# Pooled attention and a squared-ReLU feed-forward: chunk 1's softmax with tokens on partitions, weight splits shared between GpSimd and VectorE, and a unit matrix made by VectorE

## The chip, the core and the metric

The kernel runs on one core of a Trainium2 chip. The time is device microseconds of one execution of the whole program on that core; lower is better. Before the change the runs shown took 985.11, 985.27 and 3297.35 us, median 985.27.

Five engines work in parallel, each through a queue of its own in the order in which the program was written: TensorE (matrix products and transposes, PE in the profile; PEld is its loading of weights), VectorE (DVE), ScalarE (ACT), GpSimd (POOL) and SyncE (SP), which here issues all DMAs.

## What is computed

`B, H, S, D = 8, 8, 576, 64`; the model width is 8 x 64 = 512, there are 4608 tokens and 2048 hidden units. Cut to what matters:

```python
k_p = k.reshape(B, H, S // 8, 8, D).mean(axis=3)          # 72 pooled keys per head
v_p = v.reshape(B, H, S // 8, 8, D).mean(axis=3)
scores = q @ k_p.T / sqrt(D)
scores -= scores.max(axis=-1, keepdims=True)
attn = exp(scores)
attn /= attn.sum(axis=-1, keepdims=True) + 1e-9
x = (attn @ v_p).transpose(0, 2, 1, 3).reshape(4608, 512)
h = maximum(x @ w_in, 0)                                  # w_in 512 x 2048, float64
out = (h * h @ w_out).astype(float32)                     # w_out 2048 x 512, float64
```

q, k and v are float32. The two weight matrices arrive as float64, and are turned into float32 on the chip by bit operations on their 32-bit halves.

## The kernel before, in words

**Chunks, pairs and blocks.** The 4608 tokens go in 12 chunks of 384. A chunk's attention is done for four pairs of heads; pair `p` gives rows `p` of the chunk's `x`, which holds 128 features by 384 tokens for each pair. Then the feed-forward runs in 16 blocks of 128 hidden units, numbered `fc`. `hidden()` (lines 480 to 505) forms the first product of a block into a PSUM tile `h`; ScalarE takes the relu of it, and it is squared. `project()` (517 to 536) forms the second product two blocks later (`LAG = 2`) and adds it into three PSUM tiles `o`, which stay over all 16 blocks.

**Whole and split numbers.** Chunk 0 multiplies whole float32 numbers: four matmuls for a first product (`wf` by `x`, line 487), three for a second. All later chunks multiply split ones: a number is the sum of a high part of type float32r, which ScalarE makes by a copy, and a low part, which VectorE makes by a subtraction (`split`, 111 to 113). Three matmuls, high by high, high by low and low by high, stand for one (489 and 526).

**The way of a weight.** The two matrices lie in 32 keys of 128 x 512 float32: 16 of `w_in`, named `("i", column block, row block)`, and 16 of `w_out`, named `("o", fc)`. For each key the DMA brings the raw words (`land`), ScalarE writes a magnitude (`magnitude`), VectorE makes the float32 value `wf` out of it and the raw words (`to_float32`: two TENSOR_SCALAR and two SCALAR_TENSOR_TENSOR, 147 to 159; two keys that are due in one step are interleaved), and at last `split_weights` makes `wt`, high and low (161 to 163). `need` holds the step of chunk 0 in which a key is wanted, spread to at most `RATE = 2` keys in a step; a key lands `AHEAD` steps ahead of its conversion, and the first `EAGER` land at the start. Line 622 splits key `i` at step `14 + int(0.48 i)`, that is near the end of chunk 0 and in chunk 1.

**Three forms of attention.** Chunk 0 has tokens on partitions (`token_scores`, `token_normalise`, `token_turn`, 403 to 451): scores are 96 tokens by 72 keys, so that maximum and sum run along a partition, on VectorE; then TensorE turns the weights round through PSUM (`pps`), so that keys lie on partitions for the product with V (`weigh_values`). Its exponentials `te` are of scores less their maximum, a subtraction by VectorE. Chunk 1 ("early" in `scores`, 315 to 351) has keys on partitions: GpSimd finds maximum and sum over 72 partitions with PARTITION_ALL_REDUCE (`mx`, `tot`), and the sums make a round through DRAM (`rs`, `rc`, `rr`, `rd`, `rb`) so that VectorE has them on many partitions for the reciprocal. The later chunks do the same, with split K (`kh`, `kl`) and split Q (`st`).

**The order.** Every instruction but those of `make_identity` goes through the helper at line 29, which holds the order of the program; the profile so shows line 29 for nearly all of them, and they are told apart by the names of their tiles. Lines 546 to 609 write chunk 0's attention and the first tasks by hand: loads of K, Q and V of batches 0 and 1, dummy matmuls on `ident` (`keep_busy`), pooling of K by VectorE (`pool_k` for batch 0) and GpSimd (batch 1, `by_halves`), turns of K and Q on TensorE, pooling of V by matmuls with a band matrix `ones` (`pool_v_pair`, six matmuls into `vps`), and the chain from pair to pair. After it comes one loop over all 192 blocks ("steps", 653 to 674). A step issues the first product of its block, then what is due on TensorE, then the second product of two blocks ago, then the other engines' tasks of the step, the weight conversions and splits, and last the relu. What is due when is set by lists: `EARLY` for the attention of chunk 1 and `STEADY` for the later ones (the first step of each pair, and the offsets of its stages), `KV0` and `KV_AT` for loading, pooling and turning the later batches' K and V. A step before -5 counts as -5, and steps -5 to -1 come ahead of chunk 0's first block.

Of the kernel before, what the change touches and what calls it, by code (L numbers as in the profile page):

```python
# [32 lines left out]
def pooled_attn_relu2_ffn(  # L33
# [63 lines left out]
    make_identity(nc, ident)  # L97
# [43 lines left out]
    def magnitude(key):  # L141

        words = raw[key].rearrange("p a (n w) -> p a n w", w=2)
        wf[key] = half_tile("f", "wf_" + "_".join(map(str, key)))
        ACT.activation(wf[key].rearrange("p (a n) -> p a n", a=2), words[..., 1].bitcast(F32), AF.Abs)
# [169 lines left out]
    def scores(c, p):  # L315
# [3 lines left out]
        early = c == 1  # L319
        if early:  # L320

            blocks = st.rearrange("p (i t s) -> p i t s", i=2, s=QT)
            for i in range(2):
                h = 2 * p + i
                for t, (b, _, _) in enumerate(segments(c)):
                    for two in range(2):
                        rows = slice(two * D, (two + 1) * D)
                        PE.matmul(ss[two][:SP_, (i * 2 + t) * QT:(i * 2 + t + 1) * QT], lhsT=kf[b][rows, h // KH, h % KH * SP_:(h % KH + 1) * SP_],
                                  rhs=blocks[rows, i, t, :], start=True, stop=True)
        else:  # L330
            for i in range(2):
                h = 2 * p + i
                for b, o, n in segments(c):
                    kh, kl, _ = kv[b]
                    for j, kk in enumerate((kl, kh)):
                        PE.matmul(ss[i][:SP_, o:o + n], lhsT=kk[:, h * SP_:(h + 1) * SP_], rhs=st[:, i, o:o + n], start=j == 0, stop=j == 1)

        def then():
            if early:
                sc = w_tile(F32, f"sc_{c}_{p}")[:SP_, :, :CH]  # L340
                cols = sc.rearrange("p i (t s two) -> p two i t s", two=2, s=QT)
                for two in range(2):
                    ACT.copy(cols[:, two], ss[two][:SP_, :CH].rearrange("p (i t s) -> p i t s", i=2, s=QT))
            else:
# [360 lines left out]
```

## Time and profile before

| what | value |
|---|---|
| median of the runs shown | 985.27 us |
| the profiled execution | 978.9 us |
| its span, first to last instruction | 977.2 us |
| mean granted clock of TensorE | 0.997 |
| busy: TensorE, its weight loads | 947.3, 785.9 us |
| busy: VectorE, ScalarE, GpSimd | 629.2, 425.8, 401.2 us |
| first matmul of chunk 0's first product | 40.62 us |
| first matmul of chunk 1's first product | 140.10 us |

The profiled execution lies 6.4 us under the median, and its span 1.7 us under its own time. TensorE is busy for 97% of the span, so what another engine does counts only where TensorE waits for it, or where TensorE's own work changes. In the rows of the time line the figures are start, length, engine, instruction, output and inputs; "<-" in brackets names what ended the idle time before an instruction.

### The profile page before, as it was taken

How to read it: one execution, taken by the hardware profiler on the slowest of the kernel's cores; microseconds unless marked ns; L12 is line 12 of the kernel's file. 1: busy time of each engine (PE TensorE's matmuls, PEld its weight loads, DVE VectorE, ACT ScalarE, POOL GpSimd, SP SyncE). 2: the span in 40 equal slices, each digit the busy share in tenths (PEclk: the TensorE clock that was granted, in tenths of full speed). 3: DMA queues.
4: the chain of work that ended last, by engine and by line, in shares of the span. 5: the costliest groups of instructions: out<-in, count | busy, mean ns of one | idle time of the engine just before them, and what ended most of it. 6: DMA issues, size and time to landing. Idle time of an engine off the chain costs nothing.

```text
span 977.2 us, 13363 instructions
## 1 busy us (share of the span) xinstructions
PE 947.3 (97%) x4888; PEld 785.9 (80%) x4888; DVE 629.2 (64%) x1034; ACT 425.8 (44%) x847; POOL 401.2 (41%) x209
## 2 busy tenths in 40 slices
PE   6889989999999999999999999999999999999998
PEld 5544458878888888888888888888888888888997
DVE  5869997886775555776776554777677455453221
ACT  2745457674334344334434434433443434432322
POOL 4398635463444434343435335343534434340000
PEclk9999999999999999999999999999999999999999
DMA  9944203112211002112112001211221100100000
GB/s 244 354 147 163 82 17 98 49 51 82 60 56 49 25 26 74 57 52 87 49 50 74 19 23 60 66 48 36 98 57 43 58 26 17 58 10 9 33 1 32
DMA packets 53361, 64.45 MB, mean 66 GB/s; under 512 B 14936, under 2 KB 34480, under 8 KB 53296
## 3 DMA queue, kind: packets, MB, share of 16 engines
q1 hardware_dynamic: 53296, 63.61, 20.9%
q8 instruction: 38, 0.62, 0.3%
q14 instruction: 27, 0.22, 0.1%
HBM read 53.87 MB, written 9.71 MB: 65 GB/s over the span
## 4 chain that ended last, share of the span: by engine, by line
PE 77%; DVE 13%; issue 5%; ACT 4%; POOL 0%; DMA 0%; POOLq 0%; DVEq 0%; ACTq 0%; SPq 0%
PE o L29 34%; PE h L29 33%; PE sps L29 3%; PE av L29 3%; DVE wf_o L29 3%; DVE wf_i L29 2%; PE qps L29 2%; DVE st L29 2%; DVE r L29 1%; ACT st L29 1%; DVE vp L29 1%; DVE sc L29 1%; ACT gh L29 1%; DVE rb L29 1%; ACT xh L29 1%
## 5 line engine op out<-in xcount | busy, mean ns | idle before, releaser
L29 PE MATMUL h<-xh,w_i 128*128 128x384 f32 x1408 | 389.0, 337 | 0.0
L29 PE MATMUL o<-w_o,gh 128*128 128x512 f32 x1056 | 333.7, 397 | 0.0
L29 POOL PARTITION_ALL_REDUCE tot<-sc x88 | 250.2, 2890 | 192.5 <-issue 179.3
L29 PEld LDWEIGHTS h<-xh,w_i 128*128 128x128 f32 x1408 | 258.7, 188 | 8.4 <-issue 0.5
L29 POOL PARTITION_ALL_REDUCE mx<-sc x88 | 138.2, 1618 | 268.8 <-ACT sc L29 268.8
L29 PE MATMUL h<-xl,w_i 128*128 128x384 f32 x704 | 237.9, 338 | 0.0
L29 PEld LDWEIGHTS o<-w_o,gh 128*128 128x128 f32 x1056 | 193.4, 189 | 32.8 <-issue 1.2
L29 DVE TENSOR_TENSOR gl<-r,gh 128x384 fp32r<-128x384 f32 x176 | 142.6, 810 | 107.8 <-ACT gh L29 107.0
L29 PE MATMUL o<-w_o,gl 128*128 128x512 f32 x528 | 209.0, 396 | 0.0
L29 DVE TENSOR_TENSOR r<-r 128x384 f32<-128x384 f32 x160 | 101.7, 635 | 113.7 <-ACT r L29 113.2
L29 ACT CAST gh<-r 128x384 fp32r<-128x384 f32 x176 | 90.4, 514 | 179.8 <-DVE r L29 179.3
L29 ACT ACTIVATE r<-h 128x384 f32<-128x384 f32 x192 | 94.0, 490 | 106.3 <-PE h L29 105.5
L29 PEld LDWEIGHTS h<-xl,w_i 128*128 128x128 f32 x704 | 132.1, 188 | 8.2 <-issue 0.7
L29 PEld LDWEIGHTS o<-w_o,gl 128*128 128x128 f32 x528 | 99.1, 188 | 22.2
L29 ACT CAST xh<-rb 128x384 fp32r<-128x384 f32 x44 | 22.6, 513 | 136.6 <-DVE rb L29 136.6
L29 DVE TENSOR_TENSOR st<-qps,st 64x384 fp32r<-64x384 f32 x80 | 60.6, 757 | 32.6 <-ACT st L29 32.1
L29 ACT ACTIVATE sc<-sc 72x384 f32<-72x384 f32 x88 | 43.7, 525 | 74.1 <-DVE sc L29 74.1
L29 ACT CAST st<-qps 64x384 fp32r<-64x384 f32 x80 | 59.0, 738 | 0.5
L29 DVE TENSOR_REDUCE vp<-v 72x64 f32<-72x512 f32 x48 | 51.0, 1064 | 0.4
L29 DVE TENSOR_REDUCE kp<-k 96x64 f32<-96x512 f32 x42 | 44.1, 1049 | 3.7 <-DMA k<-in_k_dram 3.7
L29 DVE TENSOR_TENSOR sc<-sc,mx 72x384 f32<-72x384 f32 x88 | 44.5, 545 | 0.0
L29 DVE TENSOR_TENSOR rb<-av,rb 128x384 f32<-128x384 f32 x44 | 24.4, 555 | 30.1 <-PE av L29 29.9
(82 smaller groups left out, 725.9 us busy)
## 6 DMA issues: line engine op xcount, KB each, us to landing
k<-in_k_dram SPq DMA_DIRECT2D x48, 192.0 KB
out_dram<-ob SPq DMA_DIRECT2D x36, 256.0 KB
rb<-rd SPq DMA_DIRECT2D x88, 96.0 KB
raw_i<-in_moe_w_in_dram SPq DMA_DIRECT2D x16, 512.0 KB
raw_o<-in_moe_w_out_dram SPq DMA_DIRECT2D x16, 512.0 KB
v<-in_v_dram SPq DMA_DIRECT2D x48, 144.0 KB
q<-in_q_dram SPq DMA_DIRECT2D x30, 192.0 KB
q<-in_q_dram SPq DMA_DIRECT2D x32, 96.0 KB
```

Source lines behind the costliest of these rows:

```text
L29: return lambda *a, **k: self.tc.keep_in_program_order(f(*a, **k))
```

## The change

It has five parts.

1. VectorE makes `ident`, by a ramp that is doubled five times, a 32 x 32 transpose and four comparisons; before, GpSimd did.
2. In chunk 0, blocks from 6 on (`SPLIT = 6`) form the first product from split weights and a split `x` (`split_x0`, at step 2). Their keys are wanted one step earlier. The second product of chunk 0 stays whole.
3. The split's subtraction goes to GpSimd for those keys whose `need` lies under `HAND` (10 for `w_in`, 8 for `w_out`), 23 of 32, from one step after the conversion on; the others stay on VectorE.
4. Chunk 1 uses the softmax with tokens on partitions, without GpSimd's reductions and the round through DRAM. Its scores and turns take PSUM tiles of the pool `ps_a` (`token_banks`); chunk 0's are `ps_o` and `ps_h` as before. For both chunks ScalarE takes the exponentials straight from PSUM, 72 columns at a time, with minus the scaled maximum as its bias; VectorE's subtraction is gone.
5. Order: K of batch 1 is turned at step 0 and its V pooled at steps 1 to 4, no longer in the part ahead of chunk 0's blocks; V of batch 1 is loaded behind four keys of weights, and the first Q of chunk 1 ahead of them; `EAGER`, `AHEAD`, `EARLY`, `KV0` and `KV_AT` have other values; within a step `weigh_values` comes last of the tasks on TensorE.

```diff
-    make_identity(nc, ident)
+    DVE.memset(ident, 0.0)
+    DVE.memset(ramp[:, 0, :1], 0.0)
+    for n in (1, 2, 4, 8, 16):
+        DVE.tensor_scalar(ramp[:, 0, n:2 * n], ramp[:, 0, :n], float(n), None, op0=ALU.add)
+    DVE.transpose(ramp[:, 1, :], ramp[:, 0, :])
+    for n in range(0, P, 32):
+        rows = slice(n, n + 32)
+        DVE.tensor_scalar(ident[rows, rows], ramp[rows, 0, :], ramp[rows, 1, :1], None, op0=ALU.is_equal)
...
-    FIRST, EAGER, AHEAD = 2, 8, 5
+    FIRST, EAGER, AHEAD = 2, 11, 3
+    SPLIT, HAND = 6, {"i": 10, "o": 8}
-    KV0 = -31
-    EARLY = ((-19, -16, -13, -10), (0, 2, 3, 5, 5, 6, 7, 8))
-    KV_AT = ((0, 1, 2, 3, 4, 5), (2, 3, 4, 5, 6, 7), (5, 8), (6, 7, 8, 9, 10, 11, 12, 13))
+    KV0 = -35
+    EARLY = ((-16, -13, -10, -7), (0, 1, 2, 3, 4))
+    KV_AT = ((0, 1, 4, 5, 8, 9), (2, 3, 6, 7, 10, 11), (7, 12), (12, 13, 16, 17, 20, 21, 24, 25))
...
+    def token_banks(c, p, name, tag):
+        if c:
+            return [ps_a.tile([P, 512], F32, name=f"{name}_{c}_{p}_{j}", tag="a") for j in range(2)]
...
             for i in range(2):
-                DVE.tensor_reduce(m[:, i, 0], views[i], axis=AX.X, op=ALU.max)
+                DVE.tensor_reduce(m[:, 0, i], views[i], axis=AX.X, op=ALU.max)
+                DVE.tensor_scalar(m[:, 1, i], m[:, 0, i], -SCALE, None, op0=ALU.mult)
             for i in range(2):
-                DVE.tensor_tensor(e[i], views[i], m[:, i, 0].unsqueeze(2).to_broadcast([QT, NQ, SP_]), op=ALU.subtract)
-            for i in range(2):
-                ACT.activation(e[i], e[i], AF.Exp, scale=SCALE)
+                for t in range(NQ):
+                    ACT.activation(e[i][:, t], views[i][:, t], AF.Exp, bias=m[:, 1, i, t:t + 1], scale=SCALE)
...
+    def split_x0():
+        xts[0] = [sb.tile([P, NPAIR, CH], F32R, name=f"{x}_0", tag=x, bufs=2) for x in ("xh", "xl")]
+        split(*xts[0], x0[0])
...
-            if c == 0:
-                prods += [(wf[key][:, cols], xts[c][:, cc, :])]
+            if c == 0 and fc < SPLIT:
+                prods += [(wf[key][:, cols], x0[0][:, cc, :])]
...
     for hf in range(2):
-        transpose_k(1, hf)()
+        at(0, transpose_k, 1, hf)
         at(9 + hf, split_k, 1, hf)
+    for p in range(NPAIR):
+        at(1 + p, pool_v_pair, 1, p)
+    at(2, split_x0)
...
-        at(14 + int(i * 0.48), split_weights, key, DVE)
+        if need[key] < HAND[key[0]]:
+            at(max(need[key] + 1, i // 3), split_weights, key, GP)
+        elif key[0] == "i":
+            at(need[key] + 1, split_weights, key, DVE)
+        else:
+            at(max(need[key] + 1, NFC - 1 + late // 2), split_weights, key, DVE)
+            late += 1
```

How the instructions stand in three places, as the compiled programs hold them (helper line 29 before, 28 after). First the start. On GpSimd before, `ident` is made ahead of the band matrix `ones`:

```order
masks.py:197 MEMSET ident 128x128
masks.py:199 ISA
masks.py:199 AFFINE_SELECT ident<-ident 128x128
L29 MEMSET ones 96x432
L29 AFFINE_SELECT ones<-ones 96x432 x2
```

On VectorE after, `ident` stands ahead of the first pooled K tile (`kp`, from the loaded `k`):

```order
L28 MEMSET ident 128x128
L28 MEMSET ramp 128x1
L28 TENSOR_SCALAR ramp<-ramp 128x1
L28 TENSOR_SCALAR ramp<-ramp 128x2
L28 TENSOR_SCALAR ramp<-ramp 128x4
L28 TENSOR_SCALAR ramp<-ramp 128x8
L28 TENSOR_SCALAR ramp<-ramp 128x16
L28 STREAM_TRANSPOSE ramp<-ramp 128x32
L28 TENSOR_SCALAR ident<-ramp 32x32 x4
L28 TENSOR_REDUCE kp_0_162<-k_0_93 96x64
L28 COPY kp_0_162<-kp_0_162 96x64
```

GpSimd's three instructions became twelve of VectorE. Second, TensorE at the end of chunk 0's attention (`av` the product with V, `kps` turned K, `qps` turned Q). Before, K of batch 1 and the first Q of chunk 1 stand ahead of chunk 0's first block, and so do that pair's scores, which follow these rows:

```order
L29 MATMUL vps_3_430<-vv_3_99,ones 72x128 x6
L29 MATMUL av_2_437<-sc_2_420,vp_154 64x384 x2
L29 MATMUL pps_3_0_441<-ident,te_3_382 72x96 x4
L29 MATMUL pps_3_1_442<-ident,te_3_382 72x96 x4
L29 MATMUL av_3_463<-sc_3_451,vp_154 64x384 x2
L29 MATMUL kps_0_468<-ident,kp_0_266 128x96 x3
L29 MATMUL kps_1_473<-ident,kp_3_279 128x96 x3
L29 MATMUL qps_0_484<-ident,q_0_478 128x96 x4
```

After, the first block (`h_0`) follows the last product with V at once:

```order
L28 MATMUL av_2_445<-sc_2_436,vp_169 64x384 x2
L28 MATMUL pps_3_0_449<-ident,te_3_399 72x96 x4
L28 MATMUL pps_3_1_450<-ident,te_3_399 72x96 x4
L28 MATMUL av_3_470<-sc_3_459,vp_169 64x384 x2
L28 MATMUL h_0_497<-x_380,wf_i_0_423 128x384 x4
L28 MATMUL kps_0_506<-ident,kp_0_280 128x96 x3
L28 MATMUL kps_1_510<-ident,kp_3_293 128x96 x3
L28 MATMUL qps_0_514<-ident,q_0_105 128x96 x4
L28 MATMUL h_1_550<-x_380,wf_i_0_423 128x384 x4
L28 MATMUL vps_0_555<-vv_0_110,ones 72x128 x6
```

Turning K and Q moved from ahead of block 0 to behind it, and pooling V of batch 1 (`vps`) to behind block 1. Third, GpSimd during chunk 0's blocks. Before, it has the reductions of chunk 1's softmax behind the pooled K:

```order
L29 TENSOR_TENSOR kp_3_279<-k_4_95 96x64 x2
L29 ISA
L29 ISA mx_0_0_515<-sc_0_512 72x384 x2
L29 ISA tot_0_0_554<-sc_0_512 72x384 x2
L29 ISA mx_1_0_619<-sc_1_616 72x384 x2
L29 ISA tot_1_0_675<-sc_1_616 72x384 x2
L29 ISA mx_2_0_753<-sc_2_750 72x384 x2
L29 ISA tot_2_0_805<-sc_2_750 72x384 x2
```

After, 23 subtractions of the splits stand there, of which these are the last seven, and then the first reduction of chunk 2:

```order
L28 TENSOR_TENSOR w_o_899<-wf_o_782,w_o_899 128x512
L28 TENSOR_TENSOR w_o_968<-wf_o_782,w_o_968 128x512
L28 TENSOR_TENSOR w_i_0_971<-wf_i_0_814,w_i_0_971 128x512
L28 TENSOR_TENSOR w_i_2_1013<-wf_i_0_814,w_i_2_1013 128x512
L28 TENSOR_TENSOR w_o_1016<-wf_o_883,w_o_1016 128x512
L28 TENSOR_TENSOR w_i_0_1072<-wf_i_0_956,w_i_0_1072 128x512
L28 TENSOR_TENSOR w_i_2_1149<-wf_i_0_956,w_i_2_1149 128x512
L28 ISA
L28 ISA mx_0_0_1180<-sc_0_1179 72x384
```

The reductions of chunk 1 are gone from GpSimd, and the splits took their place. On VectorE after, between the sums of chunk 1's pair 2 and the maxima of its pair 3 (`tm_3`, from the scores `sps_3`) stand two interleaved pairs of keys with one subtraction of K's low part (`kl`) between them; the second pair:

```order
L28 TENSOR_TENSOR kl_503<-kf_505,kh_502 128x288
L28 TENSOR_SCALAR wf_i_0_956<-wf_i_0_956 128x512
L28 TENSOR_SCALAR wf_o_996<-wf_o_996 128x512
L28 TENSOR_SCALAR wf_i_0_956<-wf_i_0_956 128x512
L28 TENSOR_SCALAR wf_o_996<-wf_o_996 128x512
L28 SCALAR_TENSOR_TENSOR wf_i_0_956<-raw_i_2_885,wf_i_0_956 128x512
L28 SCALAR_TENSOR_TENSOR wf_o_996<-raw_o_886,wf_o_996 128x512
L28 SCALAR_TENSOR_TENSOR wf_i_0_956<-raw_i_2_885,wf_i_0_956 128x512
L28 SCALAR_TENSOR_TENSOR wf_o_996<-raw_o_886,wf_o_996 128x512
L28 TENSOR_REDUCE tm_3_1115<-sps_3_0_1092 96x4
```

Before, the work between conversions was chunk 1's products and reciprocals; now it is the maxima, sums and normalisation of token softmax.

More of the change, by code (lines that the diff above doesn't have):

```diff
@@ L7 @@
 from concourse import mybir
-from concourse.masks import make_identity
 from concourse._compat import with_exitstack
@@ L555, in pooled_attn_relu2_ffn @@
         load_k(1, i)
-    for p in range(NPAIR):
-        load_v_pair(1, p)
+    load_q(1, 0)
     need = {}
@@ L565, in pooled_attn_relu2_ffn @@
     first_keys = keys[:FIRST]
[L566 removed]
+    for key in keys[:FIRST + 2]:
         land(key)
[L568 removed]
+    for p in range(NPAIR):
+        load_v_pair(1, p)
+    for key in keys[FIRST + 2:EAGER]:
         land(key)
```

115 lines of the change are left out of this document (52 added, 63 removed).

## The prediction

> **What bounds the kernel now.** I read the windows by stage first, then TensorE's waits stage by stage, then the time lines of the first 150 us. Each row of windows gives the stretch, its length, the busy time of the five engines, the granted clock and the DMA.
>
> ```profile
> 0.00:40.60 40.60, 29.48 (x264) 23.68 (x264) 27.56 (x69) 17.59 (x34) 13.17 (x33) 1.00 1.01 289
> 40.60:140.10 99.50, 90.78 (x324) 46.53 (x321) 87.82 (x151) 51.11 (x102) 72.72 (x22) 0.98 0.39 130
> 140.10:215.00 74.90, 73.25 (x366) 60.56 (x365) 62.16 (x98) 51.43 (x101) 37.96 (x15) 1.00 0.20 60
> ```
>
> The kernel has three parts. Until 40.6 us chunk 0's attention runs as a chain through four engines. From 40.6 to 140.1 TensorE does chunk 0's sixteen blocks and is busy 90.8 of 99.5 us, with VectorE at 87.8 just behind it. From 140.1 on TensorE is nearly always busy. The rest is in its waits (the first three rows are of 40 to 150 us, the last of 150 us to the end):
>
> ```profile
> PE h L29 <- ACT r L29: 3.3, 2, 2.1
> PE h L29 <- DVE wf_i L29: 3.0, 5, 0.8
> PE sps L29 <- DVE st L29: 2.3, 1, 2.3
> ...
> PE sps L29 <- DVE st L29: 6.2, 8, 1.7
> ```
>
> So 8.6 us are waited for in chunk 0 and 6.2 in all later chunks. The 2.3 us wait costs more than itself, since the granted clock (column before the last two) then falls to 0.52:
>
> ```profile
> 133.30:135.60 2.30, 0.05 (x1) 0.08 (x2) 1.85 (x3) 2.27 (x5) 0.00 (x0) 1.00 0.10 28
> 135.60:138.00 2.40, 2.40 (x6) 1.58 (x7) 2.30 (x5) 2.34 (x6) 0.56 (x1) 0.52 0.03 7
> 138.00:140.10 2.10, 2.10 (x5) 0.74 (x4) 2.10 (x3) 2.07 (x5) 2.10 (x2) 0.74 0.00 0
> ```
>
> That is 2.40 x 0.48 + 2.10 x 0.26 = 1.7 us lost. Everything the change can win is in the first 140 us and in those 6.2. Nothing in the sixteen-block body of the later chunks is touched but the hours at which K and V are pooled.
>
> **The change, part by part: the start.** The rows are start, length, engine, instruction, and in brackets the idle time before it.
>
> ```profile
> 8.79 1.65 PE L29 MATMUL idle<-ident 128*128 128x128 f32 x6 [8.79 <-POOL ident masks.py:199]
> 10.23 0.69 PE L29 MATMUL kps<-ident,kp 96*128 96x96 f32 x3
> ...
> 6.79 0.19 DVE L29 COPY kp<-kp 96x64 f32<-96x64 f32 x1
> ...
> 36.55 1.57 PE L29 MATMUL av<-sc,vp 72*64 72x384 f32 x4 [0.68 <-ACT sc L29]
> 38.05 0.71 PE L29 MATMUL kps<-ident,kp 96*128 96x96 f32 x6
> ...
> 40.62 2.85 PE L29 MATMUL h<-x,wf_i 128*128 128x384 f32 x8
> ```
>
> TensorE waits for GpSimd's ident until 8.79 and turns K at 10.23, though the third pooled tile was ready at 6.98. VectorE is idle until 3.47 us, when its first K lands; twelve tiny instructions fit there, so making ident costs nothing. If K landed at once they would cost some 2 us. The gain is at most 10.23 - 6.98 = 3.2 us. Then the chain from pair to pair rules: exponentials now read PSUM in eight pieces (slower for ScalarE), but VectorE's subtraction is gone; I let these cancel. The new banks rule adds a wait: a pair's scores go into banks that ScalarE's exponentials of an earlier pair still read, with that pair's transposes queued behind on TensorE. I take 0.5 us off for it: the last values end at 38.1 - 2.7 = 35.4 (bounds 34.9 and 38.1). Pooling V of batch 1, now behind the start, lay in gaps of this chain; taking it out gains nothing there. In SP's queue V of batch 1 moves behind four weight loads and chunk 1's first Q ahead of them; it is now wanted some 25 us later, so I price this at nothing. Without that slack it would be the wait for one such load.
>
> **TensorE's work in chunk 0.** Starts of neighbouring groups give what each takes:
>
> ```profile
> 22.53 1.53 PE L29 MATMUL vps<-vv,ones 96*72 96x128 f32 x12
> 23.89 0.82 PE L29 MATMUL pps<-ident,te 96*72 96x96 f32 x8
> 24.65 1.22 PE L29 MATMUL sps<-kf,st 64*96 64x72 f32 x16
> ...
> 93.79 1.45 PE L29 MATMUL h<-x,wf_o 128*128 128x384 f32 x4
> ...
> 96.37 2.74 PE L29 MATMUL o<-wf_i,r 128*128 128x512 f32 x6
> 98.94 1.45 PE L29 MATMUL h<-x,wf_o 128*128 128x384 f32 x4
> ...
> 160.38 0.33 PE L29 MATMUL h<-xh,w_i 128*128 128x384 f32 x1
> ...
> 162.48 0.62 PE L29 MATMUL o<-w_o,gh 128*128 128x512 f32 x2
> ```
>
> A first product takes 96.37 - 93.79 = 2.58 us with whole weights and 162.48 - 160.38 = 2.10 with split ones, three matmuls for each old one; a second product takes 98.94 - 96.37 = 2.57. Ten blocks change: -4.8. Four V poolings come in from the start, 4 x 1.36 = +5.4. Four pairs of token turns are new, 4 x 0.76 = +3.0. Turning K and Q and the first scores of chunk 1 move behind block 0, 40.62 - 38.05 = +2.6. TensorE thus has 6.2 us more here. Its old work is 90.8 - 1.7 = 89.1. Without any wait chunk 1 would begin at 35.4 + 89.1 + 6.2 = 130.7 in place of 140.1. The waits decide what is left of those 9.4 us.
>
> **VectorE and GpSimd.** The first four rows are one run of VectorE and the pause after it; the next two what GpSimd and SP's queue did meanwhile. Then GpSimd's additions by shape (busy, mean ns), a 96x8 instruction of VectorE beside such additions and the same alone, and the weight conversions of the stage.
>
> ```profile
> 46.56 1.41 DVE L29 TENSOR_SCALAR wf_i<-wf_i 128x512 f32<-128x512 f32 x4
> 50.31 1.41 DVE L29 TENSOR_SCALAR wf_o<-wf_o 128x512 f32<-128x512 f32 x4
> 57.20 0.67 DVE L29 SCALAR_TENSOR_TENSOR wf_i<-raw_o,wf_i 128x512 uint32<-128x512 uint32 x1
> 65.49 0.17 DVE L29 TENSOR_SCALAR rr<-rc 96x8 f32<-96x8 f32 x1 [7.61 <-DMA rc<-rs]
> ...
> 46.81 15.95 POOL L29 PARTITION_ALL_REDUCE tot<-sc  x2 [1.67 <-ACT sc L29]
> ...
> 60.29 2.74 SPq L29 DMA_DIRECT2D rs<-tot  x2
> ...
> L29 POOL TENSOR_TENSOR k<-k 96x256 f32<-96x256 f32 x6 | 4.3, 720 | 5.8 <-DMA k<-in_k_dram 5.8
> L29 POOL TENSOR_TENSOR k<-k 96x128 f32<-96x128 f32 x6 | 2.8, 469 | 0.5
> ...
> 26.17 0.46 DVE L29 TENSOR_SCALAR tm<-tm 96x8 f32<-96x8 f32 x1
> ...
> 30.53 0.17 DVE L29 TENSOR_SCALAR tm<-tm 96x8 f32<-96x8 f32 x1
> ...
> L29 DVE TENSOR_SCALAR wf_o<-wf_o 128x512 f32<-128x512 f32 x15 | 8.7, 612 | 2.6 <-ACT wf_o L29 2.4
> L29 DVE TENSOR_SCALAR wf_i<-wf_i 128x512 f32<-128x512 f32 x14 | 8.7, 652 | 0.0
> L29 DVE TENSOR_SCALAR wf_i<-wf_i 128x512 uint32<-128x512 uint32 x14 | 8.3, 627 | 0.1
> L29 DVE TENSOR_SCALAR wf_o<-wf_o 128x512 uint32<-128x512 uint32 x15 | 7.9, 562 | 0.0
> ```
>
> Two keys take VectorE 50.31 - 46.56 = 3.75 us undisturbed, 0.35 of it per TENSOR_SCALAR. Over the stage 58 of these took 33.6 us, 13 more than 58 x 0.35: they were held up by GpSimd. The reverse is stronger. GpSimd's sum that was issued at 46.81 sent its result only at 60.29, 2.4 us after VectorE's run ended at 57.9; the run itself kept its pace. [...]
>
> Of GpSimd's new work, 23 splits of 128x512, no row stands here. From 0.720 and 0.469 the step is 0.25 per 128 columns, so 1.22 us each, 28 in all (estimate). [...] VectorE gives up 23 splits, but only three of the 32 stood in this stage before, all at its end; so this relieves the next stage and not this one. Token softmax costs it about as much as the old subtractions and products, since the reciprocal's round trip (7.61 us idle at 65.49, and 2.1 us of TensorE's wait) goes. New are x's low half over 1536 columns (four times a 384-column subtraction, about 2) and four V copies (1). VectorE so needs about 88 + 3 = 91 us, less some 6 for keys that are due after the last gating one, plus some 5 of waits for ScalarE; it starts at about 36.5, is done with block 14's weights at about 126.5, and TensorE has some 10 us left from there (two blocks of 2.10, two second products, a pair's scores): 136.5. ScalarE gets 25 casts forward from the next stage and holds chunk 1's exponentials, ordered ahead of the relu of a block: a late maximum on VectorE keeps a PSUM bank from being freed. I add 1. Chunk 1 begins at 137.5, that is 130.7 + 6.8 us of waits: 2.6 earlier.
>
> [...]
>
> **After 140 us.** 21 splits leave VectorE's next stage and K and V are pooled over twice as many blocks, both of which thin what stands ahead of st on VectorE. Of the 6.2 us of waits I take 3 as gone (bounds -6 and +4, since new hours can meet GpSimd's reductions).
>
> **The sum.** -2.6 - 3 = -5.6 us: span 971.6, profiled execution 973.3. The profiled execution before took 978.9 with a span of 977.2; the median of the runs shown is 985.27, 6.4 us above. I carry the difference over: 985.27 - 5.6 = 979.7, or 980.
>
> **Rivals.** (1) Forecast, waits of 4 to 11 us in chunk 0: 975 to 984, chance 0.48. (2) The splits cost VectorE nearly nothing, since its pauses for ScalarE and TensorE take them: waits of 1 to 3 us, chunk 1 at 132 to 134, and 4 us later on: 985.3 - 7.5 - 4 = 974, 968 at best; for it, GpSimd loses its 72.7 us of reductions in this stage; against it, VectorE's load; 0.24. (3) Slower: GpSimd is locked out, as at 46.81. [...] Blocks 8, 10 and the turns then wait 3 to 6 us each, with clock losses of 1.7 behind the longest: 14 to 21 us of waits. It is slower from 9.4 + 3 = 12.4 us on, 987 to 994; 0.18. (4) The new hours of K and V collide and cost 0.5 us in each of ten chunks: 988; 0.05. (5) It doesn't do what it says at the start, because Q and not ident holds the first transposes: 983; 0.05.
>
> About 2% (20 us) is what a measurement of this kernel tells from no change. Faster than that needs the whole 9.4, all 6.2 and 4 more: 0.03. Slower needs case 3 at its worst beside case 4: 0.03. Within 2%: 0.94. The range leaves out some 0.08 at each side, the best end of case 2 and the worst of case 3: 969 to 993.
>
> **What would show it.** Right: the first K transposes near 7 us, chunk 0's first product near 35, chunk 1's between 134 and 142, VectorE's conversions with single lengths over 1 us beside a split. Wrong: first products that wait for GpSimd's w_i by more than 4 us together (case 3), or splits of 1.2 us with no VectorE row stretched (case 2); a start later than 38 us; more than 6.2 us of waits after 150 us.

## The result: 1.4% slower

The changed kernel took 998.74 us in the median (998.34 to 1000.13) beside 985.19 us of the kernel before: a ratio of 1.0142, interval 1.0122 to 1.0162. Measured a second time it was 997.67 beside 984.57 us, 1.0141 [1.0099, 1.0184]. The prediction was 980 us with a range of 969 to 993: the sign was wrong, and the time lies outside the range.

I cut both traces at two marks: the first matmul of chunk 0's first product, and the first second product of chunk 1 ("the mark" from here on). In each row stand the stretch, its length, the busy time of TensorE, its weight loads, VectorE, ScalarE and GpSimd, and then the granted clock and the DMA. The windows of the changed kernel:

```profile
0.00:46.85 46.85, 37.29 (x190) 27.16 (x191) 27.97 (x76) 18.98 (x52) 12.70 (x31) 0.74 0.99 283
46.85:181.73 134.88, 116.84 (x524) 75.59 (x523) 107.84 (x195) 78.17 (x169) 63.42 (x31) 0.91 0.27 88
181.73:998.40 816.67, 812.90 (x4250) 714.16 (x4248) 488.33 (x773) 341.19 (x676) 300.02 (x153) 1.00 0.15 47
```

The same of the kernel before:

```profile
0.00:40.62 40.62, 29.50 (x264) 23.68 (x264) 27.58 (x69) 17.61 (x34) 13.17 (x33) 1.00 1.00 289
40.62:153.17 112.55, 103.83 (x379) 55.64 (x377) 97.50 (x168) 58.04 (x116) 78.70 (x24) 0.98 0.37 125
153.17:977.20 824.03, 813.99 (x4251) 706.58 (x4249) 504.08 (x799) 350.15 (x698) 309.35 (x152) 1.00 0.15 47
```

The start lost 6.2 us, chunk 0 lost 22.3, and all behind the mark gained 7.4: together 21.2 in one look at each. (A look is one execution.) That is more than the 13.6 us between the medians, since the look at the kernel before lies 6.3 us under its median and the one at the changed kernel 1.4 above. Two looks at the changed kernel gave spans of 998.4 and 995.9, and 134.88 and 132.22 us for chunk 0, so less than 3 us of a single look is not read; where the clock at the start comes out otherwise, it can be more (chunk 0's first product came at 40.62 us in one look at the kernel before and at 46.25 in another with an edit that does not touch the start). Chunk 1's first product, forecast at 137.5 us, came at 168.69.

Of the 22.3 us of chunk 0, 13.0 are TensorE being busy longer and 9.3 TensorE waiting longer (18.0 against 8.7). The granted clock of 0.74 and 0.91 says at once that the busy time is not all new work. Weighted with the granted clock in slices of 0.1 us, the busy time is 106.5 us of full speed against 102.1: 4.4 us are work and 8.6 are clock. TensorE's waits from 40 to 165 us in the changed kernel (total, times, longest):

```profile
PE pps L28 <- DVE te L28: 9.8, 4, 4.5
PE av L28 <- ACT te L28: 5.3, 1, 5.3
PE h L28 <- ACT r L28: 3.0, 3, 1.2
PE av L28 <- ACT sc L28: 1.3, 2, 1.0
```

The waits are in chunk 1's softmax: its turns (`pps`) wait for VectorE's normalisation, and one product with V (`av`) for ScalarE's exponentials. Behind the mark TensorE waits for nothing at all; the kernel before waited 6.2 us there.

### The profile page after: what moved, and what is told of

It is laid out like the page before. It is cut to its first block, busy times and chain, and to the rows that moved or that the text cites. A ratio compares the mean times of both kernels' runs of the same rounds, so it can differ in the third digit from the quotient of the medians.

```text
span 998.4 us, 13540 instructions
## 1 busy us (share of the span) xinstructions
PE 967.0 (97%) x4960; PEld 816.9 (82%) x4960; DVE 624.1 (63%) x1044; ACT 438.3 (44%) x896; POOL 376.1 (38%) x214
## 4 chain that ended last, share of the span: by engine, by line
PE 92%; DVE 5%; ACT 2%; issue 1%; DMA 0%; ACTq 0%; DVEq 0%
PE o L28 41%; PE h L28 39%; PE av L28 4%; PE sps L28 4%; PE qps L28 2%; DVE wf_o L28 2%; DVE wf_i L28 1%; PE vps L28 1%; DVE tm L28 1%; ACT te L28 1%; PE pps L28 1%; DVE te L28 0%; PE kps L28 0%; DVE xl L28 0%; ACT sc L28 0%
## 5 line engine op out<-in xcount | busy, mean ns | idle before, releaser
L28 PE MATMUL h<-xh,w_i 128*128 128x384 f32 x1488 | 416.4, 340 | 1.7 <-ACT r L28 1.7
L28 PEld LDWEIGHTS h<-xh,w_i 128*128 128x128 f32 x1488 | 272.8, 188 | 13.7 <-ACT r L28 4.0
L28 POOL PARTITION_ALL_REDUCE tot<-sc x80 | 200.6, 2554 | 205.3 <-issue 199.8
L28 PE MATMUL h<-xl,w_i 128*128 128x384 f32 x744 | 249.9, 336 | 0.0
L28 POOL PARTITION_ALL_REDUCE mx<-sc x80 | 116.6, 1504 | 234.2 <-ACT sc L28 227.0
L28 DVE TENSOR_TENSOR r<-r 128x384 f32<-128x384 f32 x160 | 105.7, 660 | 109.0 <-ACT r L28 108.6
L28 PEld LDWEIGHTS h<-xl,w_i 128*128 128x128 f32 x744 | 139.7, 188 | 10.1 <-issue 2.6
L28 ACT ACTIVATE sc<-sc 72x384 f32<-72x384 f32 x80 | 39.7, 525 | 44.3 <-DVE sc L28 44.3
L28 PE MATMUL av<-sc,vp 72*64 72x384 f32 (+1 forms) x256 | 47.1, 454 | 6.9 <-ACT te L28 5.3
L28 PE MATMUL o<-wf_o,r 128*128 128x512 f32 x96 | 50.7, 670 | 0.0
L28 POOL TENSOR_TENSOR w_i<-wf_i,w_i 128x512 fp32r<-128x512 f32 x14 | 25.9, 1858 | 57.3 <-ACT w_i L28 57.3
```

What stands on the lines that cost most here:

```text
L28: return lambda *a, **k: self.tc.keep_in_program_order(f(*a, **k))
```

## Experiments on the start

TensorE's time line at the start of the changed kernel:

```profile
3.38 1.65 PE L28 MATMUL idle<-ident 128*128 128x128 f32 x6 [3.38 <-DVE ident L28]
...
14.43 4.85 PE L28 MATMUL vps<-vv,ones 96*72 96x128 f32 x24
...
21.62 1.18 PE L28 MATMUL sps<-kf,st 64*96 64x72 f32 x14 [1.05 <-ACT te L28]
...
34.27 1.50 PE L28 MATMUL pps<-ident,te 96*72 96x96 f32 x8
```

Its windows of 4 us, in which the granted clock is the third column from the end:

```profile
16.00:20.00 4.00, 3.95 (x26) 3.77 (x24) 0.65 (x2) 0.35 (x1) 3.17 (x8) 1.00 1.11 267
20.00:24.00 4.00, 2.95 (x25) 2.52 (x24) 3.74 (x11) 2.28 (x10) 3.69 (x10) 0.76 1.05 380
24.00:28.00 4.00, 3.37 (x18) 2.86 (x16) 3.76 (x11) 1.76 (x5) 3.69 (x9) 0.50 1.06 271
...
44.00:48.00 4.00, 3.67 (x9) 1.44 (x8) 0.00 (x0) 2.37 (x5) 0.00 (x0) 0.50 0.43 151
48.00:52.00 4.00, 4.00 (x19) 2.48 (x18) 3.87 (x9) 2.98 (x7) 0.00 (x0) 0.83 0.13 19
```

TensorE starts at 3.38 and turns its third K tile at 6.99, near 7 us as forecast. But the 24 records of two V poolings at 14.43 take 4.85 us, and took 2.78 in the kernel before (the twelve matmuls of these two poolings show as x24 and the four of a block's first product as x8, so that the x8 of `h` is one block): TensorE still runs at half speed, though the granted clock shows as 1.00 in the window of 16 to 20 us. It comes up near 19 us (4.85 us lie between 2.78 at full speed and the 5.33 of a later look at half speed), the scores then wait 1.05 us for exponentials that still read their bank, and from 22 to 49 us the clock is at half. A turn of eight takes 1.50 us there, 0.85 in the kernel before.

**A dense first stretch:** nine dummy products in place of three.

```diff
-    IDLE = (3, 1)
+    IDLE = (9, 1)
```

> The changed kernel with nine instead of three dummy products of ident at the start (TensorE busy without a gap from 3.4 to about 8 us). Cold-start theory (TensorE's gaps of 0.6 to 0.7 us between 4.8 and 12.4 us keep its clock at half until 49.6 us): with a dense first run the clock comes up by about 8 us, the twelve matmuls of a V pooling take 1.4 us and not 2.8, and chunk 0's first product starts at 36 to 39 us in place of 46.85; span 988 to 991. Rival (the chain itself is longer: the exponentials in eight pieces, 1.77 us a pair instead of 0.8, and banks that are waited for): the first product stays behind 44 us, span 996 or more.

First product at 40.26, V poolings in 2.78 us, span 990.1; the clock fell again at 23.6 us, behind a wait of 1.69 us for `te`, until 44. So the early gaps cost something and are not the whole. The look is one of two runs of 991.8 us; the two others took 997.4 and 997.8, as long as the changed kernel. The median is 994.62 us and the ratio 1.0167 [1.0134, 1.0200], which overlaps that of the changed kernel: no gain is shown.

**ident by GpSimd again:**

```diff
-    ramp = const.tile([P, 2, 32], F32, name="ramp")
-    DVE.memset(ident, 0.0)
...
+    make_identity(nc, ident)
```

> The changed kernel with ident made by GpSimd again. Cold-start theory: TensorE starts 5.4 us later, but then finds its operands ready, runs dense as in the kernel before and is at full clock by about 12.5 us; chunk 0's first product starts at 38 to 42 us, 5 to 9 us earlier than with the early ident (46.85); span 990 to 994. Rival (chain itself longer): the late ident comes on top, first product at 48 to 52 us, span 1000 to 1004.

First product at 51.58, span 1001.9: the rival was right. The late start did not make TensorE dense: it ran at half speed until about 31 us, the waits for the exponentials are there all the same, and from 35.5 us the clock was at half again.

**Old exponentials, with the nine dummies:**

```diff
-                DVE.tensor_scalar(m[:, 1, i], m[:, 0, i], -SCALE, None, op0=ALU.mult)
             for i in range(2):
-                for t in range(NQ):
-                    ACT.activation(e[i][:, t], views[i][:, t], AF.Exp, bias=m[:, 1, i, t:t + 1], scale=SCALE)
+                DVE.tensor_tensor(e[i], views[i], m[:, 0, i].unsqueeze(2).to_broadcast([QT, NQ, SP_]), op=ALU.subtract)
+            for i in range(2):
+                ACT.activation(e[i], e[i], AF.Exp, scale=SCALE)
```

> The changed kernel with nine dummy products at the start, and the exponentials as before (VectorE subtracts the maximum out of PSUM, ScalarE takes 288 columns at once). Bank theory (a pair's scores wait 1.1 and 1.7 us for ScalarE's eight exponentials of the pair before, since these hold the bank, and these gaps let the clock fall): waits of scores for te gone, clock full from 8 us on, first product at 34 to 37 us, span 982 to 987. Filler theory: without V poolings in the chain's gaps the clock falls all the same; first product 39 to 42, span 987 to 991.

First product at 35.97, 4.3 us earlier than with the dummies alone; span 986.7. The scores' waits of 1.06 and 1.69 us shrank to 0.19 and 0.38. But the clock still fell, at 28 us, and chunk 0's first block took 5.49 us at half speed where it takes 2.85. Each theory has a part.

**V of batch 1 pooled in the gaps again, with the nine dummies** (its loads are ahead of the weights again):

```diff
-    at(1 + p, pool_v_pair, 1, p)
...
         after = [token_scores(0, p + 2), pool_v_pair(0, p + 2)] if p + 2 < NPAIR else []
+        after.append(pool_v_pair(1, p))
```

> The changed kernel with nine dummy products at the start, and V of batch 1 pooled in the gaps of chunk 0's attention again (loaded ahead of the weights), not at steps 1 to 4. With nine dummies alone the clock came up at 7 us and fell to half again from 23.7 to 44 us, chunk 0's first product started at 40.3. Filler theory (the V poolings in the gaps kept TensorE's clock up): no half clock from 24 to 44 us, first product at 35 to 38 us, and 5.4 us less TensorE work behind it; span 978 to 984. Rival (the gaps come from banks that wait for the exponentials; the poolings only fill what would be idle): clock still falls, first product at 40 to 42; span 985 to 989.

First product at 48.60, span 997.7: both wrong. Up to 12 us TensorE's instructions are those of the run with dummies alone, in the same order and some 0.5 us later, but the clock fell at 12 us here, behind waits of 0.3 to 0.6 us, and not there. It was up from 19 to 22 us, and again, with the V poolings, from 36 us, still inside the chain, until 46.

This run says little against the poolings as filler. The run with all remedies (last of the experiments on the later chunks) has nine dummies, old exponentials and the poolings in the gaps, and so differs at the start from the run with old exponentials in the poolings alone. A turn late in the chain, in the run with old exponentials and then in the one with all remedies:

```profile
31.96 1.50 PE L28 MATMUL pps<-ident,te 96*72 96x96 f32 x8
```

```profile
35.40 0.85 PE L28 MATMUL pps<-ident,te 96*72 96x96 f32 x8
```

With the poolings back the clock stayed up to the chain's end. It is one look at each.

**ident alone**, in the kernel before:

```diff
-    make_identity(nc, ident)
+    ramp = const.tile([P, 2, 32], F32, name="ramp")
+    DVE.memset(ident, 0.0)
...
```

> The kernel before with ident made by VectorE, nothing else. Cold-start theory as first put (an early start with gaps of 0.6 us leaves the clock at half): first product of chunk 0 at 43 us or later, span 979 to 986. Rival (the clock falls for the chain's gaps later on, which the poolings of V and the old exponentials fill here): TensorE warms up during the V poolings at the latest and the first product comes at 36 to 39 us; span 972 to 976.

First product at 40.36 against 40.62, between the two expectations, span 976.3 against 977.2. TensorE started at 3.38, and at 16.5 us was exactly where it had been: the 5.4 us went into three gaps of 0.7 us (pooled K twice, the load of Q once), into turns and scores at half speed, and into V poolings that took 4.32 us instead of 2.78. From there on TensorE ran at full speed.

What carries the start is seen beside two later looks at the kernel before with an edit that does not touch it (`before_last`, below). Two V poolings and a pair's scores in the first of them:

```profile
16.07 4.34 PE L29 MATMUL vps<-vv,ones 96*72 96x128 f32 x24
20.34 0.90 PE L29 MATMUL sps<-kf,st 64*96 64x72 f32 x16
```

And in the second:

```profile
14.35 5.33 PE L29 MATMUL vps<-vv,ones 96*72 96x128 f32 x24
19.61 1.56 PE L29 MATMUL sps<-kf,st 64*96 64x72 f32 x16
```

The same rows of the program reached full speed near 13 us in the look that the prediction read, at 19 in the first of these and near 27 in the second, and its first product came at 40.6, 44.7 and 46.3 us (in the first of these `ident` itself came 1.4 us later). The time at which the clock came up differs by some 14 us between these three executions. The busy stretch ahead of it differs too: in the look that the prediction read TensorE started at 8.79 us and was at full speed some 4 us later, while in the second of the later looks it is busy for all of the 18.70 us from 8.50 to 27.20 us, and runs at half speed until near 27. Nor does one length of a wait stand ahead of every fall: in chunk 0 of the changed kernel the granted clock falls 3.8 and 3.7 us into the waits of 4.5 and 5.3 us, and at the start it fell behind waits of 1.05 and 1.69 us.

What drops it there is open. The wait of 1.05 us was followed by half clock in eight looks with this start; in a ninth (`dve_x`, below) one of 1.22 us at the same place was not. Nor is it clear why the clock stayed at half from 28.5 to 39.7 us in the changed kernel, with one gap of 0.28 us in it. The rows there are of 96*72 and 72*64, but the V poolings in which it rose near 19 us are of 96*72 too; with products of 128*128 it rose 2.5 us after their start at 46.85 us, and after some 5 us in the run with old exponentials.

## Experiments on chunk 0

**The buffer of x.** The changed kernel's rows around 90 us, of TensorE, ScalarE and VectorE:

```profile
88.54 2.74 PE L28 MATMUL h<-x,wf_i 128*128 128x384 f32 x8
...
101.29 1.54 PE L28 MATMUL pps<-ident,te 96*72 96x96 f32 x8 [4.53 <-DVE te L28]
...
91.32 0.48 ACT L28 CAST xh<-av 128x384 fp32r<-128x384 f32 x1 [3.64 <-PE h L28]
...
91.83 0.56 DVE L28 TENSOR_TENSOR xl<-av,xh 128x384 fp32r<-128x384 f32 x1 [5.46 <-ACT xh L28]
...
93.64 1.76 DVE L28 SCALAR_TENSOR_TENSOR wf_o<-raw_o,wf_o 128x512 uint32<-128x512 uint32 x1
95.33 1.78 DVE L28 SCALAR_TENSOR_TENSOR wf_i<-raw_i,wf_i 128x512 uint32<-128x512 uint32 x1
...
99.99 1.61 DVE L28 TENSOR_TENSOR te<-te,tm 96x288 f32<-96x288 f32 x2
```

ScalarE cannot write chunk 1's high part (`xh`) until TensorE has finished the block at 88.54, the last that reads whole `x`. Whole `x`, its own high part and chunk 1's share two buffers, so chunk 1's takes that of whole `x`, which block 5 frees. VectorE, next in line, stands for 5.46 us; then comes a key pair, and behind it the normalisation (`te`) that TensorE's turn waits for.

```diff
-            x0.append(sb.tile([P, NPAIR, CH], F32, name=f"x_{c}", tag="xh", bufs=2))
+            x0.append(sb.tile([P, NPAIR, CH], F32, name=f"x_{c}", tag="x0", bufs=1))
```

> The changed kernel with a buffer of its own for chunk 0's whole x. Buffer theory: chunk 1's high part of pair 0 waited until block 5 had read that buffer (ScalarE 3.6 us idle, VectorE 5.5 us idle before 91.8 us); with its own buffer that pause goes, the turn of pair 1 no longer waits 4.5 us, and chunk 1 starts 5 to 8 us earlier; span 990 to 993. Rival (VectorE is late because GpSimd's splits stretch it): the pause moves on and at most 2 us are won; span 996 or more.

Span 991.7, chunk 0 up to the mark 128.19 us instead of 134.88 (132.22 in the second look), that is 6.7 or 4.0 us less. VectorE's pause shrank from 5.46 to 1.44 us and the turn's wait from 4.5 to 1.9: the theory holds.

**No split in chunk 0's blocks:**

```diff
-    SPLIT, HAND = 6, {"i": 10, "o": 8}
+    SPLIT, HAND = 16, {"i": 10, "o": 8}
...
-    at(2, split_x0)
```

> The changed kernel with whole weights and a whole x in all blocks of chunk 0 (SPLIT = 16, no split of x). Price as predicted: 4.8 us more TensorE work, but chunk 1's x no longer waits for a buffer (6.7 us in the run with a buffer of its own), so 995 to 999 against 996 to 998. Rival (splitting x and having keys a step earlier costs ScalarE and VectorE more than TensorE gains): 992 or less.

Span 993.8, between the two theories; chunk 0 took 129.99 us, 1.8 more than with the split and a buffer of its own. Beside a buffer of its own, splitting ten blocks is thus worth some 2 us at most, less than two looks can differ by, and not the 4.8 of its matmuls. With the shared buffer it costs: chunk 0 is 2.2 to 4.9 us shorter without it than in the two looks at the changed kernel. (One turn waits 5.0 us for VectorE's copy of pooled V here, and does not in the others, so the split is not the only difference.)

**All splits on VectorE:**

```diff
-    SPLIT, HAND = 6, {"i": 10, "o": 8}
+    SPLIT, HAND = 6, {"i": -9, "o": -9}
```

> The changed kernel with all subtractions of the splits on VectorE, none on GpSimd (those of w_in right behind the conversion, those of w_out from step 15 on). Port theory (GpSimd's splits hold VectorE up by about 13 us in chunk 0, rows of 0.41 and 0.68 us that take 1.5 to 1.8): VectorE has no stretched rows there and gives 8 to 9 us to the splits of w_in; span 3 to 6 us lower, 992 to 996. Rival (GpSimd takes real load off): VectorE is later than now, span 1002 to 1010.

Span 985.6, chunk 0 in 121.59 us: 13.3 shorter, the largest single effect and more than twice what the theory asked for. First VectorE's groups of the changed kernel with GpSimd's splits at their end (busy, mean ns), then those of this run, over equal work (up to 168 and to 155 us):

```profile
L28 DVE SCALAR_TENSOR_TENSOR wf_o<-raw_o,wf_o 128x512 uint32<-128x512 uint32 x30 | 24.8, 835 | 0.3
L28 DVE SCALAR_TENSOR_TENSOR wf_i<-raw_i,wf_i 128x512 uint32<-128x512 uint32 x28 | 21.3, 776 | 0.1
L28 DVE TENSOR_TENSOR te<-te,tm 96x288 f32<-96x288 f32 x8 | 5.9, 780 | 0.2
L28 DVE TENSOR_TENSOR xl<-x,xh 128x1536 fp32r<-128x1536 f32 x1 | 2.9, 2889 | 2.1 <-ACT xh L28 2.1
...
L28 POOL TENSOR_TENSOR w_i<-wf_i,w_i 128x512 fp32r<-128x512 f32 x14 | 25.9, 1858 | 57.3 <-ACT w_i L28 57.3
L28 POOL TENSOR_TENSOR w_o<-wf_o,w_o 128x512 fp32r<-128x512 f32 x9 | 20.8, 2314 | 9.9 <-ACT w_o L28 9.9
```

```profile
L28 DVE SCALAR_TENSOR_TENSOR wf_o<-raw_o,wf_o 128x512 uint32<-128x512 uint32 x30 | 21.6, 730 | 0.3
L28 DVE SCALAR_TENSOR_TENSOR wf_i<-raw_i,wf_i 128x512 uint32<-128x512 uint32 x28 | 18.6, 682 | 0.1
L28 DVE TENSOR_TENSOR w_i<-wf_i,w_i 128x512 fp32r<-128x512 f32 x16 | 10.8, 683 | 0.0
L28 DVE TENSOR_TENSOR te<-te,tm 96x288 f32<-96x288 f32 x8 | 3.3, 451 | 0.1
L28 DVE TENSOR_TENSOR xl<-x,xh 128x1536 fp32r<-128x1536 f32 x1 | 1.8, 1757 | 0.8 <-ACT xh L28 0.8
```

In these rows GpSimd's splits stretch VectorE by 5.9 (46.1 to 40.2) + 2.6 + 1.1 = 9.6 us, and over all its groups up to the mark by 13.3, while the 14 subtractions that it takes over (of the 16 in the row) cost it 9.4. So VectorE does more here in less time, 102.59 us of chunk 0 against 107.84 in the changed kernel (third figure of busy time):

```profile
46.92:168.51 121.59, 112.81 (x524) 73.40 (x523) 102.59 (x209) 73.29 (x160) 16.88 (x8) 0.94 0.31 98
```

The place counts more: of the normalisations, on which TensorE waits at once, eight took 5.9 us and not 3.3, and one pair took 2.68 us beside GpSimd and not 0.82. TensorE's waits for them fell from 9.8 to 1.9 us. (That the two engines meet at a port, as the theory's name has it, is my guess; the rows show the lengths alone.) A split alone takes GpSimd 1.26 us; the 23 took 46.7. The edit also moves nine splits of `w_out` behind the mark, with 4.9 us of ScalarE's time (78.17 to 73.29); that share is not parted from the stretching. What stands behind the mark did not grow (817.1 against 816.7 us): VectorE had room for the late splits.

**Both at once**, the two diffs of `x_own` and `all_dve`:

> All splits on VectorE and a buffer of its own for x, both at once. If the two causes are separate their gains add (12 and 6 us): span 978 to 981. If both only cure the same lateness of chunk 1's weights at the turn of pair 1, the sum falls short: 984 to 986.

Span 977.7, chunk 0 in 117.14 us: 17.7 us less than the 134.88, where the two alone make 13.3 + 6.7 = 20.0 (15.1 and 14.6 against the second look's 132.22). The causes are separate for the most part. (3.5 us of its span came from the start, where the clock rose earlier in this look.)

**The order of the products with V.** The changed rule puts them last in a step. Pair 2's then needs a bank that pair 3's scores hold, until ScalarE has read these:

```profile
136.31 1.54 PE L28 MATMUL av<-sc,vp 72*64 72x192 f32 x8 [5.26 <-ACT te L28]
...
134.58 0.44 DVE L28 TENSOR_REDUCE tm<-sps 96x4 f32<-96x288 f32 x1
...
135.32 1.77 ACT L28 ACTIVATE te<-sps,tm 96x72 f32<-96x72 f32 x8 [3.31 <-DVE tm L28]
```

The maxima stand behind two key pairs on VectorE, the exponentials behind the maxima, and TensorE behind them. Without the rule at all:

```diff
-        later = [f(*a) for f, a in sorted(((f, a) for f, a in todo if f in on_pe), key=lambda x: x[0] is weigh_values)]
+        later = [f(*a) for f, a in ((f, a) for f, a in todo if f in on_pe)]
```

> The changed kernel without the rule that the product with V comes last in a step; it so takes its PSUM bank ahead of the next pair's scores. Bank theory: the wait of 5.3 us at 131 us (product with V of pair 2, whose bank was freed only by the exponentials of pair 3) goes, with the half clock behind it; the span falls by 5 to 8 us to 990 to 993. Rival: TensorE only waits at the next place, for the relu that stands behind those exponentials on ScalarE; 2 us or less.

Span 1004.7, slower. Chunk 0 took 128.03 us, so that wait went, with a wait of 3.5 us for a relu in its place as the rival had it, but the part behind the mark took 830.58, with this in it:

```profile
PE sps L28 <- DVE st L28: 10.3, 13, 1.4
```

So the rule has two sides. Chunk 1's products first and the later ones last, beside a buffer of its own for x:

```diff
-        later = [f(*a) for f, a in sorted(((f, a) for f, a in todo if f in on_pe), key=lambda x: x[0] is weigh_values)]
+        later = [f(*a) for f, a in sorted(((f, a) for f, a in todo if f in on_pe), key=lambda x: 0 if x[0] is not weigh_values else 1 if x[1][0] > 1 else -1)]
```

> The run with a buffer of its own for x (span 991.7), and beside it chunk 1's products with V issued ahead of the next pair's scores in a step (the later chunks keep theirs last). Bank theory: the wait of 5.0 us of the product with V of pair 2 for the exponentials of pair 3 goes, and half clock behind it: span 984 to 987. Rival (the relu behind those exponentials is what counts): TensorE waits there instead, span 989 or more. Against the run without any sorting (1004.7) it also shows what the order is worth in the later chunks: they waited 10.3 us for st there and nothing in the changed kernel.

Span 987.2, just above the 984 to 987 that was expected, chunk 0 in 123.56 us against 128.19: 4.6 less. Part of the wait moved: the next turn of Q waits 2.7 us for a low part of x.

## Experiments on the later chunks

The old hours of K and V in the changed kernel:

```diff
-    KV0 = -35
+    KV0 = -31
...
-    KV_AT = ((0, 1, 4, 5, 8, 9), (2, 3, 6, 7, 10, 11), (7, 12), (12, 13, 16, 17, 20, 21, 24, 25))
+    KV_AT = ((0, 1, 2, 3, 4, 5), (2, 3, 4, 5, 6, 7), (5, 8), (6, 7, 8, 9, 10, 11, 12, 13))
```

> The changed kernel with the old hours of loading, pooling and turning K and V of the later batches (KV0 = -31 and the old KV_AT). Hours theory (the later gain of 7.3 us comes from the thinner spread): TensorE waits 3 to 6 us for st again in the later chunks, the part behind chunk 1's first second product goes from 816.7 to 820 to 824. Order theory (it comes from issuing the products with V last in a step): that part stays within 1 us of 816.7.

816.40 us behind the mark against 816.67. They do nothing.

The rule of the order alone, in the kernel before:

```diff
-        later = [f(*a) for f, a in todo if f in on_pe]
+        later = [f(*a) for f, a in sorted(((f, a) for f, a in todo if f in on_pe), key=lambda x: x[0] is weigh_values)]
```

> The kernel before with the products with V issued last in a step, nothing else. Order theory: the 6.2 us of waits of scores for st in the later chunks go, the part behind the mark falls from 824.0 to 817 to 819, span 970 to 973. Hours theory: 4 us or more of these waits stay, span 975 to 978.

```profile
44.69:153.95 109.26, 101.98 (x379) 55.23 (x377) 96.03 (x167) 58.70 (x117) 77.79 (x24) 1.00 0.34 109
153.95:969.10 815.15, 811.29 (x4250) 712.57 (x4248) 504.39 (x800) 351.85 (x698) 305.28 (x153) 1.00 0.16 48
```

815.15 us behind the mark instead of 824.03, a little better than expected. TensorE waits for nothing from 180 us on, and chunk 0 is 3.3 us shorter too (it took 110.90 in the run with `ident` alone, so perhaps only 1.6 of that come from the order). The reason is read from the order of the instructions: with the product last, the next chunk's scores get `st` before VectorE turns to the product's scaling and split. Span 969.1 although this look started 4 us late.

**A version that beats both.** Three candidates were timed: all remedies together on the changed kernel (nine dummies, V poolings in the gaps, old exponentials, a buffer of its own for x, chunk 1's products first, all splits on VectorE), each by the diff shown above; and the kernel before with the order alone, and with `ident` as well. The changed kernel was timed once more beside other runs, unedited.

> The changed kernel with five edits together: nine dummy products; V of batch 1 pooled in the start's gaps; exponentials as before (subtraction on VectorE, 288 columns at once); a buffer of its own for chunk 0's whole x, and chunk 1's products with V ahead of the next scores; all splits on VectorE. If the causes are those named (cold clock and bank gaps at the start, the buffer of x, the bank of the product with V, GpSimd's splits on the port), each goes: first product at 35 to 37 us at full clock, chunk 1's first second product (181.7 in the changed kernel, 153.2 in the kernel before) at 145 to 151, later part 817 us as in the changed kernel; span 962 to 968, a ratio of 0.980 to 0.990 to the kernel before. If something else lengthens chunk 0, that mark stays behind 158 and the span over 975.

> The kernel before with the products with V issued last, timed. If the order is the whole of the gain in the later chunks (8.9 us by the marks of one look), the ratio to the kernel before is 0.988 to 0.993; if that look was lucky, 0.995 or more.

> The same with ident made by VectorE as well. If the start is set by the chain and the loads behind it, ident brings nothing in the profile where the kernel before has ident at 8.8 us, but takes away the runs where it comes later (first product at 44.7 us in the look at the order alone): ratio 0.986 to 0.991, 1 to 4 us less than the order alone. If early gaps leave the clock at half, it is slower than the order alone.

> The changed kernel once more, unedited, beside the kernel before on this chip, where the kernel before ran in 979.4 us (985.2 earlier). If the two differ by a fixed amount, about 993 to 1000 us and a ratio of 1.014 to 1.020; if the earlier ratio was of that chip only, a ratio under 1.010.

| kernel | median, us | ratio to before, interval |
|---|---|---|
| changed, again | 997.67 | 1.0141 [1.0099, 1.0184] |
| changed, all remedies | 975.58 | 0.9930 [0.9905, 0.9955] |
| before, order alone | 968.00 | 0.9855 [0.9815, 0.9895] |
| before, order and ident | 969.40 | 0.9870 [0.9829, 0.9911] |

With all remedies the first product came at 38.42 at full clock, later than expected because a V pooling waited 2.3 us for its load; chunk 0 took 112.48 us. That is the 112.55 of the kernel before, and more than the 109.3 of the order alone: with the faults named here mended, the new chunk 0 gains nothing. This look is the fastest of eight runs (969.75 us; five took 975.6 to 976.8), and the ratio missed the 0.980 to 0.990 that was expected, so not every fault of the start or of chunk 0 is found. One line of the change, put into the old kernel, is the whole gain that these runs show. Its ratio of 0.9855 is a little under the 0.988 to 0.993 that the part behind the mark alone would give, and `ident` by VectorE adds nothing that three rounds can tell.

## Why the prediction was wrong, step by step

**The start: -2.7 us forecast, +8.8 measured.** Chunk 0's last values were to end at 35.4 us in place of 38.1. The first product, which now follows them at once, came at 46.85, and the 38.05 of the kernel before is what to hold against it. (The 6.2 us of the result are less because 2.6 us of turns and scores moved behind the first product, which the forecast counts as TensorE's work.) The step "I take 0.5 us off for it" for the new banks and the step that taking V's poolings out "gains nothing there" both looked at waits alone. In the changed kernel the waits for banks were 1.05 and 1.18 us; the clock was at half for 27. That the waits and the thinner chain cost the clock is borne out, in one look, by the run with all remedies (nine dummies, old exponentials, poolings back), whose first product came at 38.42 at full clock; which gap drops it stays open. That the exponentials "cancel" was wrong by size too: eight pieces take ScalarE 1.77 us a pair, two of 288 columns took 0.81, and the subtraction that went had freed the bank. The 3.2 us for `ident` were no gain where TensorE was at half speed: it started on time, at 3.38 us, and lost them there (4.85 us for two V poolings, 2.78 in the kernel before). That TensorE can be at half speed under a granted clock of 1.00 stood in the kernel before, where the same eight turns take 1.49 us at first and 0.82 later:

```profile
10.71 1.49 PE L29 MATMUL qps<-ident,k 96*128 96x96 f32 x8
...
20.63 0.82 PE L29 MATMUL qps<-ident,q 96*128 96x96 f32 x8
```

**TensorE's work: +6.2 forecast, +4.4 measured.** Busy time rose 13.0 us, and 8.6 of that are clock (see the result), where the forecast took off 1.7 for the old kernel and put nothing in for the new one.

**The waits: 6.8 forecast, 18.0 measured, and not where they were looked for.** The 88 us that the sum carries over for VectorE hold the 13 us by which GpSimd holds it up in the kernel before. GpSimd's splits cost it 13.3 us over all groups, so that price was right in size, but the sum spread it over VectorE's load as if only its end counted. Some of it fell on the normalisations, which TensorE waits for within a step: 9.8 of the 18.0 us. One wait was not seen at all: the shared buffer of x, 4.0 to 6.7 us with what follows from it. It is a wait for a buffer's last reader, which neither the rows of the kernel before nor the order of instructions shows; it stands in the tile's tag and count of buffers. The bank kept by a late maximum was named, at 1 us; the product with V waited 5.3 for it, and another order won 4.6 of that back.

**Rival 3** had the right sign, and its 14 to 21 us of waits hold the 18.0. Its 987 to 994 us were 5 us short, as it left the start alone, and its sign to look for, first products that wait for GpSimd's `w_i`, did not come: they waited 0.0 us. GpSimd was held up, with single splits of 4.94 us where one alone takes 1.26, and still had them ready; VectorE did not have its softmax.

**After the mark: -3 forecast, -7.4 measured.** New hours and moved splits, "both of which thin what stands ahead of st", were the wrong edits. Neither does anything that can be seen (816.4 and 817.1 against 816.7); the sort of the products with V, which the prediction did not price, does it all.

**The range** of 969 to 993 left out the worst of case 3, and no case had the start later than 38.1 us together with long waits in chunk 0. Both came, and the range had no room for that.

## What to carry to other kernels

Before an early stage is thinned or an operation is moved out of its gaps, ask whether it was what kept TensorE's clock up: read the length of equal matmuls there, not the granted clock alone (1.49 and 0.82 us here for the same eight turns, both under a granted clock of 1.00). Before a tile gets a second use, list who reads each buffer of its tag last, and when. And where work handed from a busy engine to an idle one still holds the busy one up, as GpSimd's splits did VectorE by 13.3 us, the price is paid at the instructions they happen to meet; what counts is whether these stand ahead of a wait.

## What was not expected of the hardware

With the same rows TensorE came to full speed near 13, 19 and 27 us after the program's start; between the first and the last of these looks chunk 0's first product moved by 5.6 us. In the last, TensorE was busy without a gap for 18.70 us and at half speed for nearly all of them (two V poolings took 5.33 us there and 2.78 in the first look). Waits of 1.05 and 1.69 us were followed by half clock in a thin stretch, where a wait of 1.20 us in the kernel before, amid 128x384 products, was not.
